# A tuned 2:4-sparse linear layer on one core: the order of its opening planned anew, zero products ahead of the first transposes

## The chip, the cores and the metric

The kernel runs on one core of one Trainium2 chip. The metric is device time in microseconds (us) of one execution, lower is better. The recorded median before was 234.06 us. Fast runs are undisturbed by the chip's slower state.

## The reference, cut to what matters

```python
# x: 16 x 512 x 1024, w: 1024 x 1024, b: 1024, all bf16
wg = w.reshape(256, 4, 1024)
mag = abs(wg)
thr = second largest of the four magnitudes      # cut: argsort and take_along_axis
wp = (wg * (mag >= thr)).reshape(1024, 1024)     # 2 of every 4 rows stay, per column
return einsum("bsd,df->bsf", x, wp) + b
```

The 8192 tokens are 64 tiles of 128. The weight must be pruned before any real product can start, and all of it before the first token is finished: the opening of the kernel is about feeding TensorE while that goes on.

## The kernel before: the parts that matter

VectorE prunes the weight in six pieces (`abs`, `hi`, `lo`, `t1`, `t2`, `thr`, `mask`, `mult`; the digit is the piece, 0 to 5; piece 0 arrives as four one-row loads, 1 to 3 complete the upper half of the contraction, 4 and 5 are the lower half). Eight token tiles are transposed on TensorE (`T`), copied to SBUF by ScalarE (`C`), and multiplied by each piece as it comes (`M5.0y` is tile 5, piece 0, second two rows). `F` is a run of zero products, which compute nothing and are meant to keep TensorE's clock up. `W` spreads a pruned piece over partitions by four transfers (`W1.0` is piece 4, `W1.1` piece 5); `X` and `Y` are transposing loads. `A` opens the sums of four more tiles; `close` finishes tiles, and its first one needs all of `W1.0`. Where a piece is counted in words, the count starts at one: the third piece is digit 2; the fifth is digit 4. A transfer has "landed" when its completion semaphore has been counted up in full, which is later than its last data packet.

```python
def filler(n, rep=1):
    for _ in range(n):
        pe(nc.tensor.matmul(warm_ps[:, :rep * P], lhsT=zeros[:], rhs=..., start=True, stop=True))  # cut

def spread(g, c0, c1, eng="sp"):
    for k in range(4):
        issue(eng, wp_nat[:, 4 * g + k, c0:c1], wp[32 * k:32 * k + 32, g, :, c0:c1])

psum_t = tc.tile_pool(name="psum_t", bufs=2, ...)   # two transpose buffers; psum_o has six banks (cut)
order = {
    "pe": "T7a F2 T6a T5a F8 T0a T1a M5.0y M6.0y ...  M6.3 M5.3 A1h0 A2h0 A0h0 A2h1 A3h1 A1h1 A0h1",  # cut
    "dve": "abs0a hi0a abs0b lo0a hi0b lo0b t10 t20 thr0 mask0y mult0y ... mult4 abs5 hi5 ... mult5",  # cut
    "act": "C7a C6a C5a C0a C1a C4a S0b0 ...",      # cut
    "sp": "W0.0 X0 W0.1 X1 W1.0 Y1 W1.1 Y0",
}
filler(6, 4)
filler(8)
run({eng: order[eng].split() for eng in order})
...
closes = [(8, 0), (9, 0), (10, 0), (11, 0), (5, 0), (6, 0), (7, 0), (8, 1), ...]   # cut
```

Of the kernel before, what the change touches and what calls it, by code (L numbers as in the profile page):

```python
# [10 lines left out]
def kernel(  # L11
# [241 lines left out]
    def stage(q, n):  # L253
        if (q, n // 2) not in staged:
# [3 lines left out]

    order = {
        "pe": (  # L260
            "T7a F2 T6a T5a F8 T0a T1a M5.0y M6.0y M7.0y M0.0y M5.0x M6.0x M1.0y T4a M1.0x M0.0x "
            "T3a M7.0x T2a M4.0y M4.0x M3.0x M3.0y M2.0x M2.0y M1.1y M7.1y M7.1x M5.1y M0.1y M6.1x "
            "M1.1x M3.1y M4.1x M5.1x M2.1y M2.1x M0.1x M4.1y M3.1x M6.1y M3.2 M6.2 M2.2 M1.2 M7.2 "
            "M5.2 M0.2 M4.2 M4.3 M1.3 M3.3 M0.3 M7.3 A3h0 M2.3 M6.3 M5.3 A1h0 A2h0 A0h0 A2h1 A3h1 "
            "A1h1 A0h1"
        ),
        "dve": (
            "abs0a hi0a abs0b lo0a hi0b lo0b t10 t20 thr0 mask0y mult0y mask0x mult0x abs1 hi1 lo1 "
            "t11 t21 thr1 mask1y mask1x mult1y mult1x abs2 hi2 lo2 t12 t22 thr2 mask2 mult2 lo3 hi3 "
            "abs4 t13 t23 thr3 mask3 mult3 lo4 t24 hi4 t14 thr4 mask4 mult4 abs5 hi5 lo5 t25 t15 "  # L270
            "thr5 mask5 mult5"
        ),
        "act": (
            "C7a C6a C5a C0a C1a C4a S0b0 C3a C2a S2b0 S3b0 abs3 S1b0 S1b1 S0b1 S3b1 S2b1 S0b2 S2b2 "
            "S1b2 S3b2 S3b3 S0b3 S2b3 S1b3"
        ),
        "sp": (
            "W0.0 X0 W0.1 X1 W1.0 Y1 W1.1 Y0"
# [212 lines left out]
```

## Time and profile before

| | before |
|---|---|
| time, median us | 234.06 |
| span in the profile, us | 232.3 |
| first transpose (lands with x) | 5.58 us |
| first real product | 7.56 us |
| first product that finishes a tile | 29.11 us |

From the page of the kernel before: the chain that ended last, by engine, and two groups (busy us, mean ns of one, then idle time ahead of them and what ended it).

```profile
PE 96%; DMA 2%; issue 1%; ACTq 0%; ACT 0%; DVE 0%
...
L135 PE MATMUL ps<-zeros 128*128 128x128 bf16 (+1 forms) x24 | 4.1, 328 | 1.0 <-DVE zeros L86 1.0
L191 PE MATMUL tp<-ident,x 128*128 128x128 bf16 x32 | 2.9, 220 | 1.5 <-DMA x<-in_x_dram 1.3
```

The reader is to see that the chain is TensorE for 96% of the span. Little can be won, and only ahead of some 30 us.

### The profile page before, as it was taken

To read this page: it belongs to the slowest core of one execution; us is meant where nothing else is said; L and a number is where in the kernel's file an instruction comes from. 1 tells how busy PE (TensorE), PEld (TensorE's weight loads), DVE (VectorE), ACT (ScalarE), POOL (GpSimd) and SP (SyncE) were. 2 spreads that over 40 slices of the span, in tenths; PEclk is the share of its full clock that TensorE was granted. 3 is DMA by queue.
4 is the path that set the end of the run, shared out by engine and by line. 5 is a ranking of instruction groups with operands and counts; after the bars stand their busy time and mean duration, and the time that the engine had idled before them with its cause. 6 is when DMAs were issued, how large, how long until landed. Compare 5 with 4: busy or idle time off the path is not lost.

```text
span 232.3 us, 2831 instructions
## 1 busy us (share of the span) xinstructions
PE 226.2 (97%) x1141; PEld 112.1 (48%) x1160; DVE 108.3 (47%) x185; ACT 13.6 (6%) x27; POOL 17.6 (8%) x15
## 2 busy tenths in 40 slices
PE   5999999999999999999999999999999999999995
PEld 2988444554444444444444444444444444444443
DVE  4999867854244234334334324324424424423434
ACT  2584200000000000000000000000000000000000
POOL 1000099800000000000000000000000000000000
PEclk9999999999999999999999999999999999999999
DMA  6996999995999421991239821693228922122122
GB/s 183 308 277 142 156 226 256 277 237 139 338 194 238 155 85 54 256 285 48 90 90 255 242 93 45 156 313 125 87 90 191 295 101 73 65 90 81 59 89 90
DMA packets 78268, 38.19 MB, mean 164 GB/s; under 512 B 63664, under 2 KB 70576, under 8 KB 78256
## 3 DMA queue, kind: packets, MB, share of 16 engines
q1 hardware_dynamic: 67888, 21.14, 43.5%
q10 hardware_dynamic: 10368, 16.88, 20.6%
q8 instruction: 9, 0.15, 0.3%
q14 instruction: 3, 0.02, 0.0%
HBM read 3.41 MB, written 16.78 MB: 87 GB/s over the span
## 4 chain that ended last, share of the span: by engine, by line
PE 96%; DMA 2%; issue 1%; ACTq 0%; ACT 0%; DVE 0%
PE ps L240 87%; PE ps L217 6%; DMA x<-in_x_dram 2%; PE tp L240 1%; PE tp L191 1%; ACTq L100 0%; PE ps L135 0%; ACT xt L196 0%; DVE o L400 0%
## 5 line engine op out<-in xcount | busy, mean ns | idle before, releaser
L240 PE MATMUL ps<-wp_nat,xb 128*128 128x512 bf16 (+2 forms) x832 | 178.9, 375 | 0.8
L240 PEld LDWEIGHTS <-xb 128*128 128x128 bf16 x848 | 82.4, 98 | 97.5
L400 DVE TENSOR_TENSOR o<-ps,bias_sb 128x512 bf16<-128x512 f32 (+1 forms) x112 | 71.6, 677 | 114.3 <-PE ps L240 112.0
L396 POOL TENSOR_TENSOR st<-st,bias_sb 128x1024 f32<-128x1024 f32 x8 | 16.7, 2130 | 0.0
L217 PE MATMUL ps<-wp,xt 128*128 128x256 bf16 x128 | 14.8, 273 | 0.0
L240 PE MATMUL ps<-wp_nat,xlow 128*128 128x512 bf16 x62 | 14.0, 379 | 0.1
L217 PEld LDWEIGHTS <-xt 128*128 128x128 bf16 x128 | 12.4, 98 | 1.6
L402 DVE TENSOR_TENSOR o<-ps,st 128x512 bf16<-128x512 f32 x16 | 11.1, 692 | 2.8 <-PE ps L240 2.3
L240 PE MATMUL ps<-wp_nat,xlead 128*128 128x512 bf16 x47 | 10.8, 379 | 0.1
L240 PEld LDWEIGHTS <-xlow 128*128 128x128 bf16 x64 | 7.2, 112 | 6.7
L240 PEld LDWEIGHTS <-xlead 128*128 128x128 bf16 x64 | 6.3, 98 | 7.1
L257 ACT COPY st<-ps 128x512 f32<-128x512 f32 x16 | 8.6, 593 | 5.0 <-PE ps L217 4.9
L156 DVE TENSOR_TENSOR mag<-mag,hi 128x512 bf16<-128x512 bf16 (+2 forms) x8 | 5.4, 690 | 0.2
L156 DVE TENSOR_TENSOR wp<-w_sb,mag 128x512 bf16<-128x512 bf16 (+2 forms) x8 | 5.4, 690 | 0.2
L135 PE MATMUL ps<-zeros 128*128 128x128 bf16 (+1 forms) x24 | 4.1, 328 | 1.0 <-DVE zeros L86 1.0
L191 PE MATMUL tp<-ident,x 128*128 128x128 bf16 x32 | 2.9, 220 | 1.5 <-DMA x<-in_x_dram 1.3
L240 PE MATMUL tp<-wp_nat,xlead 128*128 128x512 bf16 x16 | 4.1, 379 | 0.0
L166 DVE TENSOR_SCALAR mag<-w_sb 128x512 uint16<-128x512 uint16 (+2 forms) x6 | 2.8, 468 | 2.6 <-DMA w_sb<-in_w_dram 2.5
L135 PEld LDWEIGHTS <-zeros 128*128 128x128 bf16 x24 | 2.1, 114 | 2.6 <-issue 1.7
L156 DVE TENSOR_TENSOR hi<-mag 128x512 bf16<-128x512 bf16 (+2 forms) x7 | 3.2, 460 | 0.1
L156 DVE TENSOR_TENSOR lo<-mag 128x512 bf16<-128x512 bf16 (+2 forms) x7 | 3.2, 455 | 0.0
L191 PEld LDWEIGHTS <-x 128*128 128x128 bf16 x32 | 2.3, 114 | 1.8 <-DMA x<-in_x_dram 1.5
(16 smaller groups left out, 14.0 us busy)
## 6 DMA issues: line engine op xcount, KB each, us to landing
out_dram<-o ACTq DMA_DIRECT2D x59, 256.0 KB, 2.3
wp_nat<-wp SPq DMA_DIRECT2D x16, 128.0 KB, 3.1
w_sb<-in_w_dram SPq DMA_DIRECT2D x3, 512.0 KB, 7.1
out_dram<-o ACTq DMA_DIRECT2D x8, 128.0 KB, 1.7
x<-in_x_dram SPq DMA_DIRECT2D x3, 256.0 KB, 4.1
w_sb<-in_w_dram SPq DMA_DIRECT2D x1, 256.0 KB, 4.7
bias_sb<-in_b_dram SPq DMA_DIRECT2D x1, 256.0 KB, 7.1
w_sb<-in_w_dram ACTq DMA_DIRECT2D x2, 64.0 KB, 2.4
```

Source lines behind the costliest of these rows:

```text
L135: pe(nc.tensor.matmul(warm_ps[:, :rep * P], lhsT=zeros[:], rhs=zeros[:, None, :].to_broadcast([P, rep, P]), start=True, stop=True))
L156: dve(nc.vector.tensor_tensor(out, a, b_, op=op))
L166: dve(nc.vector.tensor_single_scalar(self.mag[:, ms, :].bitcast(u16), self.w[:, ms, :].bitcast(u16), 0x7FFF, op=Alu.bitwise_and))
L191: pe(nc.tensor.transpose(tp[:, m, :], xg[:, m, :], ident[:]))
L217: pe(nc.tensor.matmul(ps[:, c0 + d:c1 + d], lhsT=xpk[t][:, m, :], rhs=wp[:, g, m, c0:c1], start=(new and m == ms.start), stop=(left[(q, n) ...
L240: pe(nc.tensor.matmul(ps, lhsT=xt[:, kt - koff, :], rhs=wp_nat[:, kt, c0:c1], start=(kt == first), stop=(kt == last)))
L257: act(nc.scalar.copy(st[:, n % 2, :, :].rearrange("p t c -> p (t c)"), ps_open.pop((q, n))[:]))
L396: pool(nc.gpsimd.tensor_tensor(st[:], st[:], bias[:, :, None, :].to_broadcast([P, 2, 2, CW]), op=Alu.add))
L400: dve(nc.vector.tensor_tensor(o[:, c0:c1], ps, bias_sb[:, c0:c1], op=Alu.add))
L402: dve(nc.vector.tensor_tensor(o[:, c0:c1].rearrange("p (n c) -> p n c", n=2), ps.rearrange("p (n c) -> p n c", n=2), add, op=Alu.add))
```

## The change

It was meant to let TensorE start on real products sooner. All zero products stand ahead of the first transpose, where TensorE waits for x anyway, and the order of the engines is planned anew on the landing times of the four one-row loads of piece 0. No load is moved.

```diff
-            "T7a F2 T6a T5a F8 T0a T1a M5.0y M6.0y M7.0y M0.0y M5.0x M6.0x M1.0y T4a M1.0x M0.0x "
+            "F8 T7a T5a T6a T1a M5.0x M7.0x T0a M6.0x M6.0y M1.0x M7.0y M5.0y T3a M0.0y T4a M1.0y "
 (cut: the rest of TensorE's tokens, permuted)
-            "abs0a hi0a abs0b lo0a hi0b lo0b t10 t20 thr0 mask0y mult0y mask0x mult0x abs1 hi1 lo1 "
+            "abs0a hi0a abs0b lo0a hi0b lo0b t20 t10 thr0 mask0x mult0x mask0y mult0y abs1 lo1 hi1 "
 (cut)
-            "abs4 t13 t23 thr3 mask3 mult3 lo4 t24 hi4 t14 thr4 mask4 mult4 abs5 hi5 lo5 t25 t15 "
+            "t13 t23 thr3 mask3 mult3 abs5 abs4 hi4 lo4 t24 t14 thr4 mask4 mult4 hi5 lo5 t15 t25 "
 (cut: ScalarE's tokens, permuted)
```

## The prediction

> **What bounds the kernel now.** I read the page's busy shares first, then the chain that ended last, then the order of time on TensorE in the opening, then the clock of single records.
>
> The busy shares, from the page:
>
> ```profile
> PE 226.2 (97%) x1141; PEld 112.1 (48%) x1160; DVE 108.3 (47%) x185; ACT 13.6 (6%) x27; POOL 17.6 (8%) x15
> ```
>
> TensorE is busy for 226.2 of 232.3 us; no other engine reaches half. All that an order can save is therefore in the 6 us in which TensorE isn't busy, and in the zero products, which are busy but compute nothing. The chain of waits, in order of time, says where these are:
>
> ```profile
> 1.67 3.86 DMA x<-in_x_dram
> 5.53 0.05 issue
> 5.58 0.43 PE tp L191 x4
> 6.00 0.02 issue
> 6.03 0.38 ACT xt L196
> 6.41 0.04 issue
> 6.45 0.38 PE tp L191 x4
> 6.83 0.45 PE ps L135 x8
> 7.28 0.45 PE tp L191 x8
> 7.73 1.53 PE ps L217 x14
> ```
>
> The reader is to see two things. Up to 5.53 us the chain is the landing of the first tile of x, and the change moves no transfer ahead of it: that part stays. From 5.58 us on every link of the chain is TensorE, to the very end, but for one copy on ScalarE (6.03 to 6.41) and eight zero products (6.83 to 7.28). The order of time on TensorE shows the rest of the opening:
>
> ```profile
> 0.99 3.25 PE L135 MATMUL ps<-zeros 128*128 128x512 bf16 x14 [0.99 <-DVE zeros L86]
> 5.58 0.41 PE L191 MATMUL tp<-ident,x 128*128 128x128 bf16 x4 [1.34 <-DMA x<-in_x_dram]
> 5.83 0.28 PE L135 MATMUL ps<-zeros 128*128 128x128 bf16 x2
> 5.94 0.89 PE L191 MATMUL tp<-ident,x 128*128 128x128 bf16 x8
> 6.67 0.61 PE L135 MATMUL ps<-zeros 128*128 128x128 bf16 x8
> 7.12 0.61 PE L191 MATMUL tp<-ident,x 128*128 128x128 bf16 x8
> 7.56 1.69 PE L217 MATMUL ps<-wp,xt 128*128 128x256 bf16 x14
> ```
>
> TensorE waits 1.34 us for x before 5.58 us. Ten zero products (2 and 8) stand behind that point. Starts of single records show their true pace, which the overlapping durations hide: a 128-column transpose or zero product every 0.056 us, a 256-column product every 0.109, a 512-column one every 0.216. From 5.575 us (first transpose) to 29.113 us (first product of the first tile to be finished) there are 32 transposes (1.79 us), 128 piece products (13.97) and 32 opening products (6.91), together 22.67 us. The stretch takes 23.54, so 0.87 us of it is something else: 0.56 of zero products, 0.29 of idle (last transpose of the second tile issued at 6.105, next at 6.449, where 6.161 was possible), and 0.03 at the first transpose.
>
> **What the Trainium skill says.** "TensorE: Matmul & The Clock Gate", section "Wait — 56ns, not 53.3ns?", gives the start-to-start gap as N / 2.4 GHz + 2.5 ns once warm, 55.6 ns at 128 and 215.7 at 512. The trace agrees (56 and 216), which makes ten zero products worth 0.56 us. The same page, section "What's actually happening", has the clock go back to half after an idle window of about 3.4 us. In the trace the zero products switch from 107 to 56 ns at 3.8 us, and after 1.34 us of idle the transposes still run at 56; the idle will now be shorter, so I expect no cost from the clock. "Runtime: NRT & Kernel Launch", section "Instruction fetch mechanics", says that instructions come by DMA in blocks of 16 KiB, 256 instructions. The trace has this: single packets of 16,384 bytes on the instruction queue at 12.99, 27.35 and 54.48 us, later ones 27.65 us apart, which is 256 instructions (128 pairs of load and product at 0.216). This matters below.
>
> **The change, part by part.** No load is moved. The tokens are the same but for one: two of the ten zero products go, and the other eight move ahead of the first transpose.
>
> (1) Zero products. Eight more at 0.056 us from 4.07 to about 4.5 us: hidden in the wait for x, cost 0. Ten fewer behind 5.58: minus 0.56 us at most.
>
> (2) What they hid. Only two transpose buffers exist, so every third transpose waits for a copy on ScalarE (0.37 us each, from 0.26 us after the last of four transposes was issued). With the copies of before (ends 6.398, then 6.735) the new order runs: first tile 5.575 to 5.83, second to 6.05, wait until 6.449 for the first copy (0.40 idle), third tile to 6.67, wait until 6.785 for the second copy (0.12 idle), fourth tile (rows landed at 6.23) to 7.01. The first real product needs the second copy (6.735) and the first half of the first weight piece (its product, now first on VectorE, at about 6.39): it starts at 7.01, with four tiles transposed instead of five, so the idle is now 0.52 instead of 0.29 us. Sum of the opening: minus 0.56, plus 0.23 = **minus 0.33 us**.
>
> (3) Does the rest stay dense 0.33 us earlier? I walked the new order with measured durations. The half pieces arrive by 7.19 and are needed at 7.9; the second piece at 10.39 and 10.73, needed at 11.4 and 11.8; the third at 14.19, needed at 14.88; the fourth now at about 17.04 (it loses a 0.6 us step ahead of it), needed at 17.9. The copy of the eighth tile ends at about 10.90 for a product at 10.95: it just fits. Banks come free 0.4 us or more before use. So finishing would start at 28.78 instead of 29.113.
>
> (4) VectorE's order. The step "abs" of the last piece (0.6 us) moves ahead of the fifth piece. The fifth piece, done at 22.74 before, should be done at about 23.36, and the four transfers that spread it start at about 23.4 instead of 22.77. In the order of time these and the transposing load behind them were:
>
> ```profile
> 22.77 2.48 SPq L100 DMA_DIRECT2D wp_nat<-wp  x4
> 25.29 1.63 SPq L232 DMA_TRANSPOSE xlow<-in_x_dram  x1
> ```
>
> Of these four the last, issued at 24.65, landed at 29.516, 4.87 us later (the others took 2.7 to 3.0), and the product that needs it started at 29.760. So before there were only 0.24 us to spare. The cause stands in single packets: the 16 KiB fetch at 27.35 held one DMA engine for 0.93 us, with seven 1 KB packets of this transfer behind it, and the transposing load on the other engines stood still (packets of 1.9 us). The stretches show it, the last two columns being DMA share and GB/s:
>
> ```profile
> 26.00:27.40 1.40, 1.40 (x9) 0.60 (x7) 1.37 (x2) 0.00 (x0) 0.00 (x0) 1.00 0.95 216
> 27.40:29.00 1.60, 1.60 (x9) 0.77 (x8) 1.05 (x1) 0.00 (x0) 0.49 (x2) 1.00 1.57 29
> ```
>
> In the new order the demand comes 0.33 earlier (29.43 for the last quarter), the transfer is issued 0.62 later, and the fetch falls at about 27.45: it follows the program's place, 0.33 earlier and, with four rows fewer ahead, 0.43 later. If the slow engine has nine packets left then (estimate: 32 packets from 24.4 us at the 0.134 us that 25 of them took before), the transfer lands at 27.45 + 0.93 + 9 x 0.11 + 0.48 = 29.85 us: TensorE would stand for about 0.45 us. Net: minus 0.33 plus 0.45 = plus 0.12.
>
> **Rivals.** (A) The collision misses: landing by 29.4, and all 0.33 us remain, about 233.65. For it speaks that the other transfers of this kind needed 2.6 to 3.2 us (27.9 to 28.5); against it that the fetch is tied to the program's place and was there before. (B) The wait for the fifth piece takes the saving back, as worked out: about 234.1; with a worse collision, a landing near 30.2, 234.5. (C) A new wait in the opening, the tightest being the eighth copy, or a transposed tile whose landing scatters: 0.1 to 0.2 us. (D) The copies limit the start in any case: if the second ends later than 6.735, the gain shrinks one for one. (E) The weight chain becomes the bound: VectorE starts at the same landing and is earlier everywhere but for the fifth piece; I see nothing else. Even all zero products and idle time behind 5.58 us together are 0.87 us, 0.4% of the time, so no rival reaches 2%.
>
> **Range and chances.** The fast times of before are 233.77, 234.06 and 234.08 (the profiled run), mean 233.97; the 407.45 is one stray execution, which I leave out. Full saving gives 233.64, saving plus wait 234.09; about even chances give **233.9 us**. Scatter of 0.15 and a worse or missed collision give 233.3 to 234.6. Faster by over 2% would need 229.4, below what the work at its pace allows: 1%. Slower by over 2% is 238.7: 1%, for a wait that I don't see. Within 2%: 98%.
>
> **What would show it.** Step 1: no zero product behind the first transpose. Step 2: first piece product at 7.0 instead of 7.56 us, with two gaps of 0.4 and 0.12 between transposes. Step 3: TensorE dense from there to about 28.8. Step 4: the fifth piece's spread issued near 23.4 and, right or wrong, a gap before the fourth product after 28.8. The prediction is wrong if x lands at another time, if a gap opens between 7 and 28 us, or if that last gap is over 1 us.

## The result, and the profile after

The changed kernel took 234.32 us (median of 4, 234.11 to 234.55). The recorded median of the one before, 233.92, includes the stray execution; the three others were 233.52, 233.77 and 234.06. The ratio is 1.0023, 95% interval 1.0004 to 1.0043. A ratio here is the mean time of one kernel's fast runs over that of the other's of the same rounds (here 234.33 over 233.78). By the 2% rule this is "same"; it is a loss of about half a microsecond.

The page after, the lines that answer to those of before:

```profile
PE 226.5 (97%) x1139; PEld 111.9 (48%) x1158; DVE 108.0 (46%) x185; ACT 13.5 (6%) x27; POOL 17.6 (8%) x15
...
PE 85%; DVE 5%; DMA 5%; SPq 2%; issue 1%
...
L240 PE MATMUL ps<-wp_nat,xlead 128*128 128x512 bf16 x47 | 11.3, 379 | 1.0 <-DMA wp_nat<-wp 0.9
...
L135 PE MATMUL ps<-zeros 128*128 128x128 bf16 (+1 forms) x22 | 3.7, 336 | 1.0 <-DVE zeros L86 1.0
...
L191 PE MATMUL tp<-ident,x 128*128 128x128 bf16 x32 | 2.9, 221 | 0.7 <-DMA x<-in_x_dram 0.4
```

The busy shares did not move. The chain did: from 96% TensorE to 85%, and a group that had no such wait before now idles for 0.9 us on `wp_nat<-wp`, a spread. The chain in order of time names the whole path:

```profile
4.46 6.66 DMA w_sb<-in_w_dram
...
22.48 1.24 DVE wp L156
...
23.73 0.54 SPq L100
...
25.62 4.61 DMA wp_nat<-wp
30.23 0.04 issue
30.27 2.10 PE ps L240 x9
```

Up to 30.2 us the end of the kernel no longer hangs on TensorE but on the weights: the load of the third piece (landed at 11.12 us), VectorE's pruning, the issue of piece 4's spread, and 4.61 us until its last quarter landed. TensorE, in order of time:

```profile
5.04 0.69 PE L191 MATMUL tp<-ident,x 128*128 128x128 bf16 x8 [0.38 <-DMA x<-in_x_dram]
5.91 0.66 PE L191 MATMUL tp<-ident,x 128*128 128x128 bf16 x8 [0.19 <-ACT xt L196]
6.41 0.60 PE L217 MATMUL ps<-wp,xt 128*128 128x256 bf16 x4
...
8.43 0.41 PE L191 MATMUL tp<-ident,x 128*128 128x128 bf16 x4
...
27.64 1.67 PE L240 MATMUL ps<-wp_nat,xlead 128*128 128x512 bf16 x7
30.27 1.02 PE L240 MATMUL ps<-wp_nat,xlead 128*128 128x512 bf16 x4 [0.95 <-DMA wp_nat<-wp]
```

In the kernel before, the products of the same stretch stood without a wait:

```profile
27.39 4.48 PE L240 MATMUL ps<-wp_nat,xlead 128*128 128x512 bf16 x20
```

Start to start (a product's modelled end hides some of the idle time), the sums between the two traces close:

- The first transpose came at 5.04 us, 0.54 earlier: x landed at 4.99 instead of 5.53. No load was moved, and the same kernel again (e0) had it at 5.39; this is scatter between executions.
- From the first transpose to the first finishing product it is 23.47 us (5.04 to 28.51) instead of 23.54: 0.07 gained. The zero products are gone (0.56), but four transposes at 8.43 us waited 0.29 for tiles 2 and 3 of x, which landed at 8.38, the waits for copies grew from 0.29 to 0.40, and a few of 0.02 to 0.03 make up the rest.
- The fourth finishing product could have started at 29.16 and started at 30.27: 1.11 us lost.

Sum: -0.54 - 0.07 + 1.11 = +0.50 us, which is the difference of the spans (232.26 and 232.76). So a new wait has taken the gain back, and more. The early x was worth nothing here: the chain runs through the weights, and the fourth product's start alone (30.27 less 29.76) is the 0.5 us.

### The profile page after: what moved, and what is told of

The parts are those of the page before. It is cut to its first block, busy times and chain, and to the rows that moved or that the text cites. A ratio compares the mean times of both kernels' runs of the same rounds, so it can differ in the third digit from the quotient of the medians.

```text
span 232.8 us, 2828 instructions
## 1 busy us (share of the span) xinstructions
PE 226.5 (97%) x1139; PEld 111.9 (48%) x1158; DVE 108.0 (46%) x185; ACT 13.5 (6%) x27; POOL 17.6 (8%) x15
## 4 chain that ended last, share of the span: by engine, by line
PE 85%; DVE 5%; DMA 5%; SPq 2%; issue 1%
PE ps L240 85%; DMA w_sb<-in_w_dram 3%; SPq L100 2%; DMA wp_nat<-wp 2%; DVE hi L156 1%; DVE mag L156 1%; DVE wp L156 1%; DVE lo L156 1%; PE tp L240 1%; DVE mag L166 1%; DVE o L400 0%
## 5 line engine op out<-in xcount | busy, mean ns | idle before, releaser
L240 PE MATMUL ps<-wp_nat,xlead 128*128 128x512 bf16 x47 | 11.3, 379 | 1.0 <-DMA wp_nat<-wp 0.9
L196 ACT COPY xt<-tp 128x256 f32<-128x256 f32 x8 | 2.8, 376 | 3.6 <-PE tp L191 3.6
```

Of the source, the lines that this page charges most:

```text
L196: act(nc.scalar.copy(xt[:].bitcast(fp32), xpk[t].bitcast(fp32)))
L240: pe(nc.tensor.matmul(ps, lhsT=xt[:, kt - koff, :], rhs=wp_nat[:, kt, c0:c1], start=(kt == first), stop=(kt == last)))
```

## The experiments

**The theory** to be tested was the prediction's: piece 4's spread is issued later and needed earlier, so that it meets TensorE's instruction fetch, a 16 KiB packet that holds one DMA engine for about 0.9 us. (The packets' records name no engine; that packets share one is read from each starting as the one before it ends.) **Rivals:** the late issue alone is to blame; the fetch harms only together with the transposing load `Y1` behind the spread; TensorE's new order costs by itself.

For every run I took the same instants from its trace (us): when the load of the third weight piece landed, when the first of the four transfers of `W1.0` was issued, when the fetch began on its DMA engine, when the last of the four landed, how long that is from the first issue, and TensorE's extra start-to-start time ahead of the products that needed it.

| trace | third piece lands | `W1.0` issued | fetch | last landed | issue to landing | gap |
|---|---|---|---|---|---|---|
| before | 10.76 | 22.77 | 27.35 | 29.52 | 6.75 | 0 |
| after | 11.12 | 23.73 | 28.35 | 30.23 | 6.49 | 1.11 |
| e0, after again | 11.57 | 24.18 | 28.63 | 30.46 | 6.28 | 0.90 |
| e1, after, abs5 late | 11.95 | 23.96 | 28.64 | 30.53 | 6.56 | 0.58 |
| e2, after, 8 zero products fewer | 11.47 | 24.09 | 29.76 | 28.70 | 4.62 | 0 |
| e3, after, 8 more | 10.92 | 23.54 | 26.47 | 29.31 | 5.77 | 0 |
| e4, before, abs5 early | 11.63 | 24.25 | 27.23 | 29.97 | 5.71 | 0.33 |
| e5, before, zero products moved only | 11.33 | 23.35 | 28.90 | 28.08 | 4.73 | 0 |
| e6, after, `Y1` behind `W1.1` | 10.90 | 24.20 | 27.96 | 30.64 | 6.44 | 0.62 |
| e7, e2 and e1 together | 10.67 | 22.69 | 28.39 | 27.36 | 4.68 | 0 |
| e8, before, 8 fewer | 11.18 | 23.19 | 29.04 | 27.96 | 4.77 | 0 |
| e9, after, 16 fewer | 10.62 | 23.33 | 32.67 | 28.12 | 4.79 | 0 |
| e10, e7 and abs4 on ScalarE | 11.40 | 22.84 | 28.77 | 27.73 | 4.88 | 0 |
| e11, e10 again | 11.63 | 22.91 | 28.67 | 27.67 | 4.75 | 0 |

The table falls into two halves without overlap. In the seven traces whose fetch began after the last landing, the spread took 4.6 to 4.9 us. In the seven whose fetch began before it, 5.7 to 6.8. Since a late landing itself puts a trace into the second half, the fetch is better held against the first issue: 2.9 to 4.7 us after it in the seven long ones, 5.5 to 9.3 in the seven short ones, again without overlap. Each row is one execution.

**e0: the changed kernel again**, with five rounds beside the experiments e1 to e3.

> The changed kernel once more, for a ratio on the same chip as the experiments. All theories: the gap of TensorE before the fourth product of the first finished tile is there again (1.1 us in the first profile, 0.6 to 1.3 here), and the time is 0.1 to 0.3% above the kernel before (234.1 to 234.6 us).

Measured: median 234.72 us, ratio 1.0036 (1.0019 to 1.0053), a little above the expected band; the gap was 0.90 us. TensorE near it:

```profile
28.09 1.67 PE L240 MATMUL ps<-wp_nat,xlead 128*128 128x512 bf16 x7
30.51 1.24 PE L240 MATMUL ps<-wp_nat,xlead 128*128 128x512 bf16 x5 [0.74 <-DMA wp_nat<-wp]
```

What follows: the loss and its gap are there again, so the wait in the first profile was no accident.

**e1: abs5 put back.**

```diff
-  ... mult3 abs5 abs4 hi4 lo4 t24 t14 thr4 mask4 mult4 hi5 ...
+  ... mult3 abs4 hi4 lo4 t24 t14 thr4 mask4 mult4 abs5 hi5 ...
```

> The changed kernel with one step of VectorE put back: abs5 stands behind mult4 again. Theory (the spread of the fifth weight piece is issued too late, and so runs into the instruction fetch): mult4 ends at about 23.1 instead of 23.7 us, the four transfers are issued 0.6 us earlier, the last lands at 27.7 to 28.5 instead of 30.2, no gap of TensorE over 0.1 us near 29 us, and the time is 233.2 to 233.8 us, at or below the kernel before. Rival (the transfer is held until about 30 us whenever it is issued): landing near 30, gap of 1 us, 234.3 us.

Measured: 234.29 us, ratio 1.0019 (1.0006 to 1.0031); in the mean 0.41 us less than e0 (234.37 and 234.78). The expectation failed: the time stays above the kernel before, and in the profiled execution `W1.0` was issued at 23.96 instead of 23.1, since the third weight piece landed at 11.95, later than in any other trace. VectorE waited for it, and then TensorE for VectorE:

```profile
11.97 0.43 DVE L166 TENSOR_SCALAR mag<-w_sb 128x1024 uint16<-128x1024 uint16 x1 [1.56 <-DMA w_sb<-in_w_dram]
```

```profile
12.83 1.69 PE L217 MATMUL ps<-wp,xt 128*128 128x256 bf16 x14
15.44 1.81 PE L217 MATMUL ps<-wp,xt 128*128 128x256 bf16 x15 [0.91 <-DVE wp L156]
```

The second fence is TensorE of the same run: 0.91 us idle at 15.44 us on `wp`, 1.08 counted start to start. What follows: undoing this part alone does not take back the loss; the 0.41 us lies within the scatter of e0's runs (234.10 to 235.55), and this profile can't tell the theory from the rival, since the spread was issued as late as in the changed kernel. It shows a second limit, though. The landing of the load with the third piece scatters from 10.62 to 11.95 us over the fourteen traces. In the five where it came at 11.47 or later, TensorE stood for 0.29 to 1.08 us near 15 us (e0, e1, e2, e4, e11); in the nine up to 11.40 it did not.

**e2: eight zero products fewer** ahead of x, in a stretch where TensorE waits anyway. That shifts nothing but the program's place.

```diff
 filler(6, 4)
-filler(8)
```

> The changed kernel with eight zero products fewer in the hidden wait for x (none of the rest moves), so that TensorE's instruction fetch, which falls every 256 instructions, comes 16 instructions later: 8 products, 1.7 us, at about 30 instead of 28.35 us. Theory (fetch and transposing load together hold the completion of the transfer): the last quarter lands at about 28.5, no gap, 233.2 to 233.8 us. Rival (the late issue alone, without the fetch, makes the landing late): landing near 30.2, gap of about 1.1 us, 234.3 us.

Measured: 233.66 us (233.39 to 233.79), ratio 0.9987 (0.9975 to 0.9999); all five runs lie below all six of e0, and the means differ by 1.15 us. The four transfers were issued from 24.09 us on, later than in the first profile of the changed kernel, yet the last landed at 28.70. TensorE, and the stretches (sums of busy us with counts for TensorE, weight loads, VectorE, ScalarE and GpSimd; then granted clock, DMA share, GB/s):

```profile
27.13 1.03 PE L240 MATMUL tp<-wp_nat,xlead 128*128 128x512 bf16 x4
28.00 3.18 PE L240 MATMUL ps<-wp_nat,xlead 128*128 128x512 bf16 x14
```

```profile
27.40:29.00 1.60, 1.60 (x9) 0.73 (x8) 1.48 (x2) 0.00 (x0) 0.03 (x1) 1.00 0.95 220
29.00:31.00 2.00, 2.00 (x11) 0.88 (x9) 0.91 (x2) 0.00 (x0) 2.00 (x2) 1.00 0.79 168
```

The same stretches of the changed kernel:

```profile
27.40:29.00 1.60, 1.60 (x9) 0.74 (x8) 1.16 (x1) 0.00 (x0) 0.38 (x2) 1.00 1.98 149
29.00:31.00 2.00, 1.05 (x6) 0.41 (x5) 0.32 (x1) 0.00 (x0) 2.00 (x2) 1.00 0.62 138
```

The reader is to see TensorE's 2.00 us instead of 1.05 in the second stretch, and in the first that the DMA engines moved more (220 GB/s instead of 149) while being "busy" half as much: in a share of 1.98 much of the packets' time is standing still. What follows: removing work that was hidden made the kernel faster, with a late issue left in place. This speaks for the fetch and against the late issue alone.

**e3: eight zero products more** (`filler(16)` for `filler(8)`).

> The changed kernel with eight zero products more in the hidden wait for x: the fetch comes 1.7 us earlier, at about 26.6 us, before the transposing load has started to move data. Theory: no hold of all engines, but 0.9 us of one engine; the last quarter lands at 28.5 to 29.4, gap 0 to 0.3 us, 233.3 to 234.0 us. Rival (late issue alone): landing near 30.2, gap of about 1.1 us, 234.3 us.

Measured: 233.93 us, ratio 1.0002 (0.9989 to 1.0015), landing at 29.31, no gap: as the theory had it, and 0.83 us below e0 in the mean. The profiled execution hides part of it: its zero products ran at 107 ns up to 5.43 us, so that the first transpose came only at 5.77, though x had landed at 4.96. What follows: moving the fetch the other way helps too; early in the spread it costs about 1 us of the landing, late in it up to 2. And since eight products more help as eight fewer do, it isn't fewer zero products as such.

**e4: the kernel before with abs5 early**, right behind `mult3`, and nothing else.

> The kernel before with only one thing of the change: abs5 ahead of the fifth piece (right behind mult3). TensorE's order is that of before. Theory: mult4 ends 0.6 us later (about 23.4), the last quarter of its spread lands near 30 us, where it is needed at 29.76; a gap of 0.3 to 0.8 us, 234.2 to 234.7 us. Rival (the loss comes from the new TensorE order alone): no gap, 233.95 us.

Measured: 233.83 us, ratio 0.9983 (0.9947 to 1.0019; two runs of the kernel before were at 235.4 and 236.1). The trace has the landing (29.97) and a gap of 0.33 us, as the theory says; the time does not show it. What follows: the wait comes with TensorE's old order too, and e2 had the new order without it, so the new order alone is not the cause. That the early `abs5` alone makes the wait is not shown: the third piece landed at 11.63 here, and the spread was issued at 24.25, where `abs5` by itself would have given about 23.4. The expected 234.2 to 234.7 us were not seen.

**e5: only the zero products moved**, in the kernel before.

```diff
-"T7a F2 T6a T5a F8 T0a T1a M5.0y ...
+"F8 T7a T6a T5a T0a T1a M5.0y ...
```

> The kernel before with only the zero products moved: eight ahead of the first transpose, none behind, the rest of the order as before. Theory (the copies on the scalar engine set the pace of the opening): the first piece product starts 1.95 us after the first transpose instead of 1.99, so only some 0.04 us is gained; time within 0.1 us of before, but for the place of the fetch (four instructions earlier in the program). Rival (the zero products cost what they last): 1.43 us after the first transpose, 0.56 us gained, 233.4 us.

Measured: 234.06 us, ratio 0.9992 (0.9956 to 1.0028). It fits the 0.04 us of the theory; the rival's 0.56 us (0.24%) is at the lower side of the interval and can't be excluded by it. The trace is no judge of the size, since this execution had TensorE at half speed up to about 6.9 us:

```profile
2.67 2.77 PE L135 MATMUL ps<-zeros 128*128 128x512 bf16 x18
5.23 1.96 PE L191 MATMUL tp<-ident,x 128*128 128x128 bf16 x16
7.37 0.38 PE L191 MATMUL tp<-ident,x 128*128 128x128 bf16 x4 [0.18 <-ACT xt L196]
```

Sixteen transposes took 1.96 us here; and still the last tile waited for a copy on ScalarE (0.18 on the page's count, 0.34 start to start). What follows: the copies can hold the opening with no zero product in it. Inconclusive for the size.

**e6: the transposing load moved away from the fetch.**

```diff
-"W0.0 X0 W0.1 X1 W1.0 Y1 W1.1 Y0"
+"W0.0 X0 W0.1 X1 W1.0 W1.1 Y1 Y0"
-closes = [(8,0), (9,0), (10,0), (11,0), (5,0), (6,0), (7,0), (8,1), (9,1), (10,1), (11,1), (5,1), ...
+closes = [(8,0), (9,0), (10,0), (11,0), (8,1), (9,1), (10,1), (11,1), (5,0), (6,0), (7,0), (5,1), ...
```

> The changed kernel with the first low transposing load issued behind the sixth piece's spread instead of ahead of it, and the second halves of tiles 8 to 11 finished ahead of tiles 5 to 7, so that the fetch at about 28.4 us meets no transposing load. Theory: no packets of 1.5 us or more near 28 us, the last quarter of the fifth piece's spread lands at 28 to 29 us, no gap at its use; 233.3 to 233.8 us. Rival (late issue or fetch alone): landing near 30 and a gap of about 1 us, 234.3 us or more.

Measured: 234.34 us, ratio 1.0001 (0.9962 to 1.0041; with the two high runs of the kernel before). The landing was at 30.64 with no transposing load under way (one had landed at 24.71, the next was issued at 31.58), and the gap was there:

```profile
28.77 1.46 PE L240 MATMUL ps<-wp_nat,xlead 128*128 128x512 bf16 x6
30.68 2.10 PE L240 MATMUL ps<-wp_nat,xlead 128*128 128x512 bf16 x9 [0.45 <-DMA wp_nat<-wp]
```

In single packets: the 16 KiB fetch began at 27.96 and lasted 1.51 us, all other engines had finished this spread by 28.37, and seven packets of 1 KB followed on the one engine from 29.46 to 30.19. A second fetch, of 8 KiB, ran from 29.06 to 29.57. What follows: a late landing needs no transposing load in flight; the fetch with packets of the spread behind it is enough. Whether that also holds for the changed kernel is not shown, since there no packet stood behind the fetch (see the end of the next section). The same trace has tile 2 of x landing late, at 9.32 us:

```profile
9.37 0.41 PE L191 MATMUL tp<-ident,x 128*128 128x128 bf16 x4 [1.04 <-DMA x<-in_x_dram]
```

**e7: both cures**, e2's and e1's.

> The changed kernel with both cures: eight zero products fewer (fetch 1.7 us later) and abs5 behind mult4. Theory: with the fetch out of the way the earlier issue adds nothing more, the time is that of e2 (233.4 to 233.8 us). If instead the gap near 15 us (third weight piece late) or the fifth piece still cost something, e7 is 0.1 to 0.4 us below e2.

Measured: 233.83 us (233.15 to 234.39), ratio 0.9983 (0.9946 to 1.002), not clear of noise. In the trace `W1.0` was issued at 22.69 and had landed at 27.36, a microsecond before the fetch: no gap.

**e8: eight zero products fewer in the kernel before**, a control for e2.

> The kernel before with eight zero products fewer in the hidden wait for x, a control for e2. Theory (the fetch costs the changed kernel because its transfer is issued later and needed earlier; the kernel before had 0.24 us to spare): no gap either way near 29 us, time within 0.15 us of before (ratio 0.9993 to 1.0007). Rival (fewer zero products, or another place of the fetch, help any kernel of this kind): 0.3 us faster as in e2, ratio 0.9987.

Measured: 235.24 us, ratio 1.0021 (0.9978 to 1.0063). In this call the runs of the kernel before itself lay from 233.62 to 235.95 us. The profiled execution, 233.57 us, had no gap and the landing at 27.96. Inconclusive in time: whether the kernel before gains from the shift stays open.

**e9: all sixteen small zero products gone.**

```diff
-filler(8)
-"F8 T7a T5a ...
+"T7a T5a ...
```

> The changed kernel with all sixteen small zero products gone, so that the fetch comes 3.4 us later than in it, clear of the fifth piece's spread in every execution. Theory: landing 4.6 to 4.7 us after the first of the four issues, no gap at its use, 233.4 to 233.8 us, unless TensorE's clock, with some 2 us of idle in the opening, comes up later (transposes and products at 107 and 213 ns for longer): then up to 0.5 us more. Rival (e2 was chance): 234.3 us.

Measured: 234.73 us, ratio 0.9991 (0.9947 to 1.0035). Fetch at 32.67, landing 4.79 us after the first issue, no gap: the theory's trace. But TensorE ran at half speed up to 7.9 us, which the expectation had as its exception. That the missing zero products were the reason is not shown: e5, with sixteen small ones ahead of x, ran at half speed up to about 6.9 us, and e8, with none of them there, was at full speed in its first transposes (5.09 us).

**e10 and e11: a try at a version that beats both**: e7, with `abs4` on ScalarE ahead of its stage copies.

```diff
-dve: ... mult3 abs4 hi4 ...           act: ... abs3 S3b1 ...
+dve: ... mult3 hi4 ...                act: ... abs3 abs4 S3b1 ...
-pe:  M0.2 M3.2 M7.2 M1.2 M2.2 ...
+pe:  M0.2 M3.2 M1.2 M2.2 M7.2 ...
```

> A try at a version better than both: e7 (eight zero products fewer, abs5 late) with the step abs4 on the scalar engine, ahead of its stage copies, and two piece products exchanged for the later bank. Theory: VectorE saves 0.6 us ahead of the fifth piece, mult4 ends at 22.1 to 22.9 us, no gap near 29 us, 233.3 to 233.8 us; the remaining loss is the landing of the third weight piece (a gap of 0 to 1 us near 15 us), which nothing here changes. If the stage copies come too late for their banks: a gap of 0.1 to 0.5 us near 16 to 18 us, and no gain over e7.

> e10 once more, because the runs of the kernel before in its call scattered from 233.6 to 236.0 us, so that the ratio of 0.995 there may be the others' scatter and not e10's gain. If e10 is a real gain of the size that its trace allows (no gap near 29 us, up to 0.35 us in the opening), the ratio on a quiet call is 0.997 to 0.9995, 233.2 to 233.8 us; if it was only the scatter, 0.9995 to 1.001.

Measured: e10 233.62 us, ratio 0.995 (0.9913 to 0.9987), in the call where the kernel before scattered; e11, the same kernel in a quiet call, 233.83 us, ratio 1.001 (0.9975 to 1.0046), with one run at 235.9. Both traces have `mult4` done by 22.9 us, the spread landed before 27.8 and no gap at it; what they lost, they lost to loads: 0.88 us at 9.33 for tiles 2 and 3 of x (e10), 0.88 us at 15.12 for the third weight piece (e11). What follows: the wait is absent in both traces, and e11 suggests that e10's ratio was mostly the others' scatter. No version here is shown to beat the kernel before by more than e2's 0.13%.

## Why the prediction was right, point by point

- **The total.** 233.9 was forecast with 233.3 to 234.6; 234.32 was measured, inside the range and on the side of the prediction's second rival (234.1, at worst 234.5). "Plus 0.12", the sum with the wait, was about 0.4 too small (0.23% of 233.9 is 0.54), about as much as the landing was later than forecast.
- **Its own signs of being wrong.** It named three, and all three came in the first trace after: x landed at another time (4.99 us), a gap opened between 7 and 28 us (0.29 at 8.43), and the last gap was over 1 us (1.11). The forecast of the total holds; the path to it does so only in part.
- **Zero products hidden, copies in their place.** Right in kind: none behind the first transpose, and waits of 0.35 and 0.05 us between transposes in the changed kernel (the first 0.40 in e0), where 0.40 and 0.12 were forecast. The first product came 1.37 us after the first transpose (6.41 less 5.04), against 1.43 forecast.
- **"Does the rest stay dense."** Wrong in part. The walk took each landing from one trace as fixed. Tiles 2 and 3 of x cost 0.29 us in the first trace after and 1.20 in e6; the third weight piece cost 0.29 in e0. So of the 0.33 us only 0.07 were there in the first trace. The rival "a new wait in the opening" named this, at 0.1 to 0.2 us: too small. No cost from TensorE's clock was expected, and the first trace had none, but in e0 the first three transposes still ran at 107 ns.
- **The fifth piece's spread.** The step that carried the forecast, and its direction was right: issued at 23.73 (23.4 forecast; the third piece's load had landed 0.36 later than before, so rival (E), the weight chain, had a part in it by a load that it didn't name), landed at 30.23 (29.85), a gap before the fourth finishing product. Its size was off: 1.11 us against 0.45, since the product was ready at 29.16 and not at 29.43 (x landed early), and the landing was 0.38 later. Issue to landing came out as forecast (6.49 against 6.45 us), but by luck: nine packets were to stand behind the fetch, and in this trace none did.
- **The fetch.** 27.45 was forecast from the program's place; it began at 28.35, and between 26.47 and 32.67 over the runs. It moves with the place (8 products fewer: 29.76; 16 fewer: 32.67; 8 more: 26.47), but e7, also with 8 fewer, had it at 28.39, and the kernel before and e5, whose programs differ by two products, at 27.35 and 28.90. What else sets its start is open.
- **"The transposing load on the other engines stood still"** is true of the packets, before and after. e6 shows that a delay can come without one; it doesn't show that the standing load had no part in the changed kernel.
- **Small readings.** The spread's packets began at 23.98 before, so 0.62 later is 24.6 and not 24.4, which leaves about eleven packets by the same estimate, not nine. TensorE's pace changed at 3.7 us, not 3.8, and the chain "to the very end" closes with 0.29 us of VectorE.

What stays open: which of the two holds the landing in the changed kernel. In single packets the delay has two forms. In e3, e4 and e6, packets of the spread came after the fetch, and the landing followed the last semaphore packet by 0.45 to 0.54 us, much as in the seven undelayed traces (0.35 to 0.59). In the first trace after, e0 and e1, the fetch began only when the spread's packets were over (last semaphore packet 28.344, fetch 28.350 in the first), yet the landing came 1.84 to 1.89 us after that packet. There 21 packets of the transposing load stood for 1.4 to 2.0 us, and the landing followed 0.07 to 0.11 us after the last of these had ended (30.13 and 30.23 in the first). The kernel before had both. That the fetch and the starting transposing load together hold the landing is thus likely in the changed kernel, but no run separates them there.

## What to carry to other kernels

Where a kernel is bound by one engine, a saving ahead of a critical transfer also brings its demand forward: look up how long each awaited transfer had landed before its use (here 0.24 us), and expect anything saved beyond that to turn into a wait. Plan an order on the scatter of the landings, not on one trace: here it was 1.3 us for one weight piece and over 1 us for two tiles of x, each some four times what the order was to gain. When a transfer lands late for no reason of its queue, look in the packets for an instruction fetch on the same DMA engine; a few instructions more or less in idle time move it, though not to a place that these runs let one foresee (e2 and e7, with the same products removed, had it at 29.76 and 28.39).

## What the Trainium skill lacked or had wrong

- "Runtime: NRT & Kernel Launch", section "Instruction fetch mechanics", calls the cost of crossing a 16 KiB boundary "one DMA tail-bump, mostly hidden". In the traces here one such fetch held a DMA engine for 0.88 to 1.51 us; with it a transfer took 5.7 to 6.8 us instead of 4.6 to 4.9, and TensorE waited up to 1.11 us for that. The page doesn't say that it shares the DMA engines with the kernel's own transfers.
- "TensorE: Matmul & The Clock Gate", section "What you observe", puts the change to full speed "around 4µs into sustained matmul activity, ±500ns run-to-run". Here, with products from 0.99 us on, it came at 3.7 us in the kernel before (2.7 us into activity), after 5.4 in e3 (4.4) and at about 6.9 in e5 (5.9) with no idle time ahead of the transposes; in e9, with an idle stretch of 1.15 us, after 7.9 us.
- No page that I found tells what such a fetch does to a transposing load. In the five traces where it began 0.4 to 0.7 us after the load's first packet (before, after, e0, e1, e9), 21 or 22 of the load's packets took 1.3 to 2.0 us; in the six where it began 1.5 us or more after it (e2, e5, e7, e8, e10, e11), no packet of `Y1` took over 0.2 us.
